# Two shifted bit patterns by one integer addition on GpSimd, in a two-block attention kernel

## The chip, the cores and the metric

The kernel runs on one core of one Trainium2 chip. The metric is the device time of one execution in microseconds. A core has TensorE (matrix products, written to PSUM), VectorE, ScalarE and GpSimd, each with its own queue of instructions worked off in order; they wait for each other by semaphores. DMAs are issued here from the queue of the sync engine. In the profile TensorE is PE (PEld is its loading of weights), VectorE is DVE, ScalarE is ACT, GpSimd is POOL and the sync engine is SP.

## The reference

Two attention blocks stand side by side. Both take x (2048 rows of 512) and weights in bfloat16, and have 32 heads of 16 channels. A is linear attention, B is full softmax attention. The two outputs are put together along the channels, to 2048 x 1024.

```python
def _A_ref(x, wqkv, wo):
    ...                                            # q, k, v: (B, H, S, Dh) from x @ wqkv
    phi = lambda t: jnp.where(t > 0, t + 1, jnp.exp(t)) + 1e-6
    pq, pk = phi(q), phi(k)
    kv = jnp.einsum("bhsd,bhse->bhde", pk, v)
    z = jnp.einsum("bhsd->bhd", pk)
    num = jnp.einsum("bhqd,bhde->bhqe", pq, kv)
    den = jnp.einsum("bhqd,bhd->bhq", pq, z)[..., None] + 1e-6
    o = num / den
    return (lambda x, *d: x.transpose(*d))(o, 0, 2, 1, 3).reshape(B, S, D) @ wo

def _B_ref(x, wqkv, wo):
    ...
    scores = jnp.einsum("bhqd,bhkd->bhqk", q, k) * scale     # scale = 16 ** -0.5
    p = _softmax(scores, axis=-1)
    o = jnp.einsum("bhqk,bhkd->bhqd", p, v)
    return (lambda x, *d: x.transpose(*d))(o, 0, 2, 1, 3).reshape(B, S, D) @ wo
```

B has by far the most work: 32 heads x 2048 x 2048 scores, each of which needs an exponential.

## The kernel before

The kernel is written as a planner. While the program is built, it keeps a clock for each engine, guesses how long each instruction takes (the numbers beside an engine's name, in us), and decides greedily which piece of work each engine does next. The order that comes out is fixed in the program; on the chip only semaphores hold it together. So a change of the guessed durations, or of which engine does what, gives another order and another division of the work.

B's scores are cut into blocks of 128 keys by 512 queries of one head. A unit is four heads (of one parity e_ within a group Gp of eight heads), one quarter of the queries, and all keys: 64 blocks. There are 32 units. Four heads' scores are made side by side in the array, 32 rows each. To take one head of a pair out of 32 rows, K lies masked: KM holds K with the rows of the other parity set to zero.

```python
    ABL = (3, 2)          # banks of the two PSUM tiles pS that ScalarE works on
    NDG = 4               # pattern buffers
    SHIFTS = (343, 685)
    VSCALE = (203.0 / 256.0, 161.0 / 256.0)
```

A block goes one of two ways. ScalarE takes three or two blocks in one exponential, from pS to PT (fp16):

```python
                    sch.add("act", lambda e: e.activation(PT[:, row, c0:c0 + w], SCR[sl][:, 0:w], ACTF.Exp, scale=SC),
                            reads=skeys(sl), writes=[("PT", row, sl)])
```

Or VectorE makes the exponential from bits: a multiply-add of a score from a bank of pD, converted to a 16-bit integer, read as fp16, is a rough exponential. Two more patterns, the same bits plus 343 and plus 685, multiplied by scaled copies of V (VSCALE), even out its error. So such a block has three products with V (vk is 0, 1, 2), and a block of ScalarE's has one.

```python
                    sch.add("dve", lambda e: e.tensor_scalar(DI[:, buf, 0, i * 512:(i + n) * 512], DB[:, bi * 512:(bi + n) * 512],
                                                             ESC, EB, op0=ALU.mult, op1=ALU.add), ...)
# ---- cut ----
            def shift(k_):
                def go(st_, en_):
                    sch.add("dve", lambda e: e.tensor_scalar(DI[:, buf, k_, 0:n * 512], DI[:, buf, 0, 0:n * 512], SHIFTS[k_ - 1], None, op0=ALU.add), ...)
# ---- cut ----
                        sch.add("pe", lambda e, g=g, vk=vk, c0=c0, P=P, first=first, last_=last_: e.matmul(
                            PVb[32 * g:32 * g + 17, 0:512], lhsT=VV[:, Gp % 2, vk, c0:c0 + 17], rhs=P,
                            start=first, stop=last_, tile_position=(0, 32 * g)), ...)
```

How many blocks go the second way is not fixed: the planner takes one whenever a bank of pD and a pattern buffer (DI) are free and VectorE's backlog is under 6 us.

```python
        def d_backlog(at):
            return max(0.0, T["dve"] - at) + sum(c_[3] for c_ in cands["dve"])
```

The masked K of all but the first head group is made by GpSimd from a copy (KR) of the projection:

```python
            st.append(("dve", 0.6, f_ev("dve", lambda e, bk: e.tensor_copy(KR[:, kr, :], f32v(bk)), [], [("KR", kr)])))
            for e_ in range(2):
                st.append(("pool", 1.7, f_op("pool", lambda e, e_=e_: e.tensor_scalar(KM[:, r, e_, cs], KR[:, kr, :], PAR[:, e_:e_ + 1], None, op0=ALU.mult), ...)))
```

At a unit's end VectorE transposes the products, takes the reciprocal of the sums and multiplies:

```python
            st = [("dve", 0.25, f_op("dve", lambda e: e.reciprocal(zr, o[:, :, 16]), ...)),
                  ("dve", 0.4, f_op("dve", lambda e: e.tensor_tensor(xn[:, :, 16 * e_:16 * e_ + 16], o[:, :, 0:16],
                                                                      zr.unsqueeze(2).broadcast_to([128, 16, 16]), op=ALU.mult), ...))]
```

A's work lies as small jobs between B's. Its K and V are made for 16 row tiles, in two halves of 256 columns each, and kept in KNa and VNa for the sums over the rows:

```python
                return e.matmul(f32v(bk)[:, 256 * k_:256 * k_ + 256], lhsT=xTa[:, cc, t * 128:(t + 1) * 128],
                                rhs=Wa[:, cc, 512 + 512 * k_ + 256 * hp:512 + 512 * k_ + 256 * hp + 256], start=(cc == 0), stop=(cc == 3))
```

Of the kernel before, what the change touches and what calls it, by code (L numbers as in the profile page):

```python
# [231 lines left out]
def bass_concat_heads__linear_attn_block__softmax_full_mha__prompt_kernel(nc, A_x, A_wqkv, A_wo, B_x, B_wqkv, B_wo, out):  # L232
# [4 lines left out]
    NT = S // 128  # L237
# [6 lines left out]
    NDG = 4  # L244
# [17 lines left out]
    with es:  # L262
# [12 lines left out]
        WOb = sb("WOb", [128, 4, 512], BF)  # L275
# [5 lines left out]
        DI = sb("DI", [128, NDG, 3, 1024], I16)  # L281
        KR = sb("KR", [128, 2, 512], BF)
        ON = sb("ON", [128, NT, 512], BF)
        KNa = sb("KNa", [128, NT, 256], BF)
        VNa = sb("VNa", [128, NT, 2, 129], BF)
# [67 lines left out]
        load(WOb[:], B_wo.rearrange("(c p) n -> p c n", p=128), ["WOb"])  # L353
# [25 lines left out]
        for r_ in range(2):  # L379
            sch.add("pool", lambda e, r_=r_: e.memset(  # L380
                VV[:, r_, 0, :].rearrange("p (h c) -> p h c", c=17)[:, :, 16:17], 1.0), writes=[("VV1", r_)])
        mk_ident(identf, "identf")
        band(BMk, 8, 16, "BMk")
        sch.add("pool", lambda e: e.memset(VNa[:, :, :, 128:129], 1.0), writes=["VNa1"])
# [49 lines left out]
        P1, SH = (0.61, 1.12), (0.21, 0.345)  # L434
        SLK = 0.0
        PVR, PVMIN, PVURG = 3, 6, 24
# [30 lines left out]
        krc = [0]  # L467

        def proj_job(Gp, sc, kind, fast=False, **kw):
            def mm(e, bk, cc):  # L470
                return e.matmul(f32v(bk), lhsT=Wb[:, cc, kind * 512 + Gp * 128:kind * 512 + Gp * 128 + 128],  # L471
                                rhs=xTb[:, cc, sc * 512:(sc + 1) * 512], start=(cc == 0), stop=(cc == 3))
            r = Gp % 2
            cs = slice(sc * 512, (sc + 1) * 512)
            st = halves(mm, [("Wb", kind, Gp)] + [("xTb", t) for t in range(4 * sc, 4 * sc + 4)])
            needs = [("xTb", t) for t in range(4 * sc, 4 * sc + 4)]
            if Gp >= 2:
                needs.append(("filled", Gp - 2))
            if kind == 0:
                st.append(("dve", 0.6, f_ev("dve", lambda e, bk: e.tensor_copy(QT[:, r, cs], f32v(bk)), [], [("QT", r, sc)])))  # L480
                return Job(st, needs, [(2, ("Q", Gp, sc))], rel=2, **kw)
            if fast:
                for e_ in range(2):
                    st.append(("dve", 0.66, f_ev("dve", lambda e, bk, e_=e_: e.tensor_scalar(KM[:, r, e_, cs], f32v(bk), PAR[:, e_:e_ + 1], None, op0=ALU.mult),  # L484
                                                 [("PAR", e_)], [("KM", r, e_, sc)])))
                return Job(st, needs, [(2, ("K", Gp, 0, sc)), (3, ("K", Gp, 1, sc))], rel=3, **kw)
            kr = krc[0] % 2
            krc[0] += 1
            st.append(("dve", 0.6, f_ev("dve", lambda e, bk: e.tensor_copy(KR[:, kr, :], f32v(bk)), [], [("KR", kr)])))  # L489
            for e_ in range(2):  # L490
                st.append(("pool", 1.7, f_op("pool", lambda e, e_=e_: e.tensor_scalar(KM[:, r, e_, cs], KR[:, kr, :], PAR[:, e_:e_ + 1], None, op0=ALU.mult),  # L491
                                             [("PAR", e_), ("KR", kr)], [("KM", r, e_, sc)])))
            return Job(st, needs, [(3, ("K", Gp, 0, sc)), (4, ("K", Gp, 1, sc))], rel=2, **kw)
# [81 lines left out]
        def akv_job(t, hp, **kw):  # L575
            def mm(e, bk, i):
                k_, cc = divmod(i, 4)
                return e.matmul(f32v(bk)[:, 256 * k_:256 * k_ + 256], lhsT=xTa[:, cc, t * 128:(t + 1) * 128],  # L578
                                rhs=Wa[:, cc, 512 + 512 * k_ + 256 * hp:512 + 512 * k_ + 256 * hp + 256], start=(cc == 0), stop=(cc == 3))
            st = halves(mm, ["Wa", ("xTa", t)], n=8, parts=2, dur=0.11)  # L580
            st += phi_stages(0, 256, KNa[:, t, :], [("KNa", t)])
            st.append(("dve", 0.34, f_ev("dve", lambda e, bk: e.tensor_copy(VNa[:, t, :, 0:128], f32v(bk)[:, 256:512].rearrange("p (b n) -> p b n", n=128)),
                                        [], [("VNa", t)])))
            return Job(st, [("xTa", t)] + ([("akv", hp - 1, bl) for bl in range(2)] if hp else []),
                       [(5, ("ak", hp, t))], **kw)

        def akvsum_job(hp, bl, **kw):
            bq = 2 * hp + bl
            def mm(e, bk, t):
                return e.matmul(f32v(bk, 129), lhsT=KNa[:, t, bl * 128:(bl + 1) * 128], rhs=VNa[:, t, bl, :], start=(t == 0), stop=(t == NT - 1))  # L590
            st = halves(mm, [("KNa", t) for t in range(NT)] + [("VNa", t) for t in range(NT)] + ["VNa1"], n=16, parts=4, dur=0.06)
            st.append(("dve", 0.25, f_ev("dve", lambda e, bk: e.tensor_tensor(RHA[:, bq, 0:128], f32v(bk, 128), BMk[:], op=ALU.mult), ["BMk"], [("RHA", bq)])))
            st.append(("dve", 0.15, f_ev("dve", lambda e, bk: e.tensor_tensor(
                RHA[:, bq, 128:136], ZMk[:], bk[0][:, bk[2] + 128:bk[2] + 129].broadcast_to([128, 8]), op=ALU.mult), ["ZMk"], [("RHZ", bq)])))
            return Job(st, [("ak", hp, t) for t in range(NT)], [(3, ("akv", hp, bl)), (5, ("rha", bq))], **kw)
# [47 lines left out]
        kst = lambda i: [("KNa", 2 * i), ("KNa", 2 * i + 1)]  # L643
        KNf = KNa[:, :, :].rearrange("p (s b) n -> p s (b n)", b=2)
# [3 lines left out]
        def omm_job(ab, t, o2, needs, gives, lane="dve", **kw):  # L648
# [5 lines left out]
            def fin(bk):  # L654
# [4 lines left out]
                       needs + ([("akv", 1, bl) for bl in range(2)] if o2 else []), gives, **kw)  # L659
# [47 lines left out]
        def qk_reads(bl):  # L707
            res = []
            for u, j, g in bl:
                Gp, c, e_ = unit(u)  # L710
                res += [("QT", Gp % 2, c), ("KM", Gp % 2, e_, j // 4)]
# [19 lines left out]
        def d_backlog(at):  # L731
            return max(0.0, T["dve"] - at) + sum(c_[3] for c_ in cands["dve"])

        grp = {"n": 0, "open": False}
# [64 lines left out]
        def shifts(buf):  # L799
# [5 lines left out]
            def shift(k_):  # L805
                def go(st_, en_):
                    sch.add("dve", lambda e: e.tensor_scalar(DI[:, buf, k_, 0:n * 512], DI[:, buf, 0, 0:n * 512], SHIFTS[k_ - 1], None, op0=ALU.add),  # L807
                            reads=[("DI", buf, 0, i) for i in range(n)], writes=[("DI", buf, k_, i) for i in range(n)])
                    for i in range(n):
                        done(buf, k_, i, en_)  # L810
                    if k_ == 1:
                        push("dve", en_, 1, SH[n - 1], shift(2))
                return go
            push("dve", s_["t"], 1, SH[n - 1], shift(1))
# [147 lines left out]
        def unit_done(u, t_):  # L962
# [9 lines left out]
                  ("dve", 0.4, f_op("dve", lambda e: e.tensor_tensor(xn[:, :, 16 * e_:16 * e_ + 16], o[:, :, 0:16],  # L972
# [60 lines left out]
        for hp in range(2):  # L1033
            for t in range(NT):
                ajobs.append(akv_job(t, hp))
            for bl in range(2):
                ajobs.append(akvsum_job(hp, bl))
# [52 lines left out]
        while True:  # L1090
# [12 lines left out]
            if fa is not None:  # L1103
                fao = pe_opt(fa[0], 0, fa[1], fa[2], None, "q")
                opts.append(fao)
            fd = fill_d_cand()
            if fd is not None:
                opts.append(pe_opt(fd[0], 3, fd[1], fd[2], None, "q"))
            elif not d_open():
                close_group()  # L1110
            lim = max(T["act"] + sum(exps) - fa[1] - PH - LAT - SLK, fa[0]) if fa is not None and nfill[0] >= 2 else None
# [108 lines left out]
```

## Time and profile before

| | |
|---|---|
| time, median of three runs | 790.32 us (789.88 to 794.22) |
| span of the profiled execution | 795.4 us |
| mean granted TensorE clock | 0.949 |

In a line of the page's costliest groups stand: the line of the source, the engine, the operation, what it writes and reads by the program's names (buffer numbers left out), the shapes, the count; then the busy time in us and the mean ns of one; then the idle time of the engine just before these instructions, and what ended most of it. pS and pD are the PSUM tiles of scores, pPV that of the products with V, PT ScalarE's exponentials, DI the bit patterns, VV the copies of V, OT, ZR and ON a unit's outputs, KNa, VNa, EA and PQT tiles of A. In a list of waits stand the engine and its instruction, whom it waited for, and the total us, the times and the longest us. L871 is ScalarE's exponential, L783 VectorE's multiply-add, L807 its two shifts, L704 the scores' matmuls, L946 the products with V, L491 GpSimd's masking of K.

The busy times of records that overlap are counted once, so a group's busy time is less than count times mean. The end of a matmul is modelled.

### The profile page before, as it was taken

To read this page: it belongs to the slowest core of one execution; us is meant where nothing else is said; L and a number is where in the kernel's file an instruction comes from. 1 tells how busy PE (TensorE), PEld (TensorE's weight loads), DVE (VectorE), ACT (ScalarE), POOL (GpSimd) and SP (SyncE) were. 2 spreads that over 40 slices of the span, in tenths; PEclk is the share of its full clock that TensorE was granted. 3 is DMA by queue.
4 is the path that set the end of the run, shared out by engine and by line. 5 is a ranking of instruction groups with operands and counts; after the bars stand their busy time and mean duration, and the time that the engine had idled before them with its cause. 6 is when DMAs were issued, how large, how long until landed. Compare 5 with 4: busy or idle time off the path is not lost.

```text
span 795.4 us, 14718 instructions
## 1 busy us (share of the span) xinstructions
PE 687.2 (86%) x6195; PEld 213.9 (27%) x6244; DVE 666.0 (84%) x1368; ACT 733.4 (92%) x679; POOL 43.2 (5%) x41
## 2 busy tenths in 40 slices
PE   7889988888889889888888888988888888888876
PEld 4234432222223333222223222222122222221211
DVE  5989897888978887999988799889778987877971
ACT  6999998899999997999999899979899988998894
POOL 1000011110000002210000001130000000000000
PEclk9999998999999999989999799999689999988996
DMA  9900000000000000000000000000000020000000
GB/s 202 222 2 1 2 1 1 2 1 1 2 1 1 1 2 1 1 14 15 21 7 1 15 23 18 1 8 21 14 14 1 8 47 22 7 27 1 28 1 31
DMA packets 32712, 15.69 MB, mean 20 GB/s; under 512 B 24960, under 2 KB 32128, under 8 KB 32640
## 3 DMA queue, kind: packets, MB, share of 16 engines
q1 hardware_dynamic: 31840, 14.29, 7.6%
q8 instruction: 51, 0.84, 0.5%
q10 hardware_dynamic: 800, 0.39, 0.2%
q14 instruction: 21, 0.17, 0.1%
HBM read 4.72 MB, written 4.19 MB: 11 GB/s over the span
## 4 chain that ended last, share of the span: by engine, by line
ACT 60%; PE 27%; DVE 10%; issue 1%; DMA 1%; SPq 1%; DVEq 0%
ACT PT L871 59%; PE pPV L946 9%; PE pS L704 7%; DVE DI L783 5%; PE pD L704 2%; DVE DI L807 2%; PE pD L471 2%; PE pD L578 2%; PE pD L652 2%; PE pD L599 1%; ACT EA L569 1%; DMA xTb<-in_B_x_dram 1%; PE pD L549 1%; SPq L342 1%; DVE PQT L572 0%
## 5 line engine op out<-in xcount | busy, mean ns | idle before, releaser
L871 ACT ACTIVATE PT<-pS 128x1536 f16<-128x1536 f32 x624 | 719.7, 1316 | 45.8 <-PE pD L704 27.6
L783 DVE TENSOR_SCALAR DI<-pD 128x512 int16<-128x512 f32 (+1 forms) x468 | 323.7, 708 | 59.0 <-PE pD L704 53.1
L704 PE MATMUL pS<-QT,KM 32*128 32x512 bf16 x1559 | 247.8, 399 | 69.5 <-ACT PT L871 65.4
L946 PE MATMUL pPV<-PT,VV 128*17 128x512 f16 x1559 | 249.4, 399 | 0.6 <-ACT PT L871 0.5
L946 PE MATMUL pPV<-DI,VV 128*17 128x512 f16 x1467 | 223.0, 400 | 2.2 <-DVE OT L966 1.8
L807 DVE TENSOR_SCALAR DI<-DI 128x1024 int16<-128x1024 int16 (+1 forms) x490 | 192.5, 424 | 5.0
L704 PE MATMUL pD<-QT,KM 32*128 32x512 bf16 x489 | 176.2, 396 | 10.3 <-DVE DI L783 7.0
L704 PEld LDWEIGHTS pS<-QT,KM 32*128 32x128 bf16 x1559 | 58.5, 91 | 287.0 <-ACT PT L871 236.4
L946 PEld LDWEIGHTS pPV<-PT,VV 128*17 128x17 bf16 x1559 | 50.6, 89 | 68.9 <-issue 56.4
L491 POOL TENSOR_SCALAR KM<-KR,PAR 128x512 bf16<-128x512 bf16 x24 | 39.5, 1657 | 491.1 <-DVE KR L489 477.9
L946 PEld LDWEIGHTS pPV<-DI,VV 128*17 128x17 bf16 x1467 | 45.9, 89 | 66.7 <-issue 46.0
L704 PEld LDWEIGHTS pD<-QT,KM 32*128 32x128 bf16 x489 | 40.9, 91 | 58.8 <-DVE DI L783 28.9
L966 DVE STREAM_TRANSPOSE OT<-pPV 128x512 f32<-128x512 f32 x32 | 22.8, 712 | 20.0 <-PE pPV L946 19.7
L578 PE MATMUL pD<-Wa,xTa 128*128 128x256 bf16 x256 | 37.7, 275 | 1.9 <-DVE DI L783 1.5
L471 PE MATMUL pD<-xTb,Wb 128*128 128x512 bf16 x104 | 32.3, 402 | 6.1 <-DVE DI L783 2.4
L569 ACT ACTIVATE EA<-pD 128x256 bf16<-128x256 f32 (+1 forms) x48 | 25.8, 538 | 0.0
L578 PEld LDWEIGHTS pD<-Wa,xTa 128*128 128x128 bf16 x256 | 20.4, 97 | 19.2 <-issue 8.5
L549 PE MATMUL pD<-Wb,xTb 128*128 128x128 bf16 x256 | 19.4, 223 | 2.3 <-DVE KM L484 1.0
L599 PE MATMUL pD<-xTa,Wa 128*128 128x512 bf16 x54 | 16.6, 388 | 2.7 <-DVE DI L783 1.4
L652 PE MATMUL pD<-WOa,ONT 128*128 128x512 bf16 x49 | 15.8, 396 | 3.2 <-issue 2.3
L549 PEld LDWEIGHTS pD<-Wb,xTb 128*128 128x128 bf16 x256 | 14.8, 99 | 9.9 <-issue 3.1
L652 PE MATMUL pD<-WOb,ON 128*128 128x512 bf16 x52 | 14.3, 407 | 3.4 <-DVE ON L977 2.7
(82 smaller groups left out, 259.1 us busy)
## 6 DMA issues: line engine op xcount, KB each, us to landing
out_dram<-OB SPq DMA_DIRECT2D x16, 128.0 KB, 1.7
out_dram<-KNa SPq DMA_DIRECT2D x16, 128.0 KB, 1.7
Wa<-in_A_wqkv_dram SPq DMA_DIRECT2D x1, 1536.0 KB, 8.3
Wb<-in_B_wqkv_dram SPq DMA_DIRECT2D x2, 384.0 KB, 5.4
Wb<-in_B_wqkv_dram SPq DMA_DIRECT2D x1, 512.0 KB, 4.5
WOb<-in_B_wo_dram SPq DMA_DIRECT2D x1, 512.0 KB, 9.2
WOa<-in_A_wo_dram SPq DMA_DIRECT2D x1, 512.0 KB, 10.0
ON<-in_B_x_dram ACTq DMA_DIRECT2D x1, 256.0 KB, 4.3
```

Source lines behind the costliest of these rows:

```text
L471: return e.matmul(f32v(bk), lhsT=Wb[:, cc, kind * 512 + Gp * 128:kind * 512 + Gp * 128 + 128], rhs=xTb[:, cc, sc * 512:(sc + 1) * 512], st ...
L491: st.append(("pool", 1.7, f_op("pool", lambda e, e_=e_: e.tensor_scalar(KM[:, r, e_, cs], KR[:, kr, :], PAR[:, e_:e_ + 1], None, op0=ALU.m ...
L549: return e.matmul(f32v(bk)[:, tl * 128:(tl + 1) * 128], lhsT=xTb[:, cc, t * 128:(t + 1) * 128], rhs=Wb[:, cc, 1024 + Gp * 128:1024 + Gp * ...
L569: ("act", 0.051 + n * 0.000833, f_ev("act", lambda e, bk: e.activation(EA[:, q, 0:n], f32v(bk)[:, c0:c0 + n], ACTF.Exp), [], [("EA", q)])),
L578: return e.matmul(f32v(bk)[:, 256 * k_:256 * k_ + 256], lhsT=xTa[:, cc, t * 128:(t + 1) * 128], rhs=Wa[:, cc, 512 + 512 * k_ + 256 * hp:51 ...
L599: return e.matmul(f32v(bk), lhsT=Wa[:, cc, bq * 128:(bq + 1) * 128], rhs=xTa[:, cc, sc * 512:(sc + 1) * 512], start=(cc == 0), stop=(cc == 3))
L652: return e.matmul(f32v(bk), lhsT=src, rhs=WO[:, hb, :], start=(hb == 0), stop=(hb == 3))
L704: return e.matmul(dst, lhsT=KM[32 * g:32 * g + 32, Gp % 2, e_, j * 128:(j + 1) * 128], rhs=QT[32 * g:32 * g + 32, Gp % 2, c * 512:(c + 1) ...
L783: sch.add("dve", lambda e: e.tensor_scalar(DI[:, buf, 0, i * 512:(i + n) * 512], DB[:, bi * 512:(bi + n) * 512], ESC, EB, op0=ALU.mult, op ...
L807: sch.add("dve", lambda e: e.tensor_scalar(DI[:, buf, k_, 0:n * 512], DI[:, buf, 0, 0:n * 512], SHIFTS[k_ - 1], None, op0=ALU.add), reads= ...
L871: sch.add("act", lambda e: e.activation(PT[:, row, c0:c0 + w], SCR[sl][:, 0:w], ACTF.Exp, scale=SC), reads=skeys(sl), writes=[("PT", row, ...
L946: sch.add("pe", lambda e, g=g, vk=vk, c0=c0, P=P, first=first, last_=last_: e.matmul(PVb[32 * g:32 * g + 17, 0:512], lhsT=VV[:, Gp % 2, vk ...
```

## The change

The change moves the two shifts from VectorE to GpSimd. A pair of 16-bit patterns lies in a 32-bit lane; one 32-bit integer addition of a constant that holds the shift twice adds it to both, as the patterns are positive and no carry crosses. One instruction makes both shifted copies of up to two blocks: the source is read twice by a broadcast, and the constants lie in the small tile SHC. It is there to free VectorE for more blocks, and so to take blocks off ScalarE.

GpSimd's earlier work is moved to make room: the masked K is now written by eight small DMAs of 16 partitions each, over zeros set once at the start. The multiplication at a unit's end goes to GpSimd. A's K and V are made in quarters of 128 columns, two row tiles at a time, so that KNa and VNa take half the room; B's output weights are loaded late into VNa's place. The room goes to six pattern buffers instead of four. The planner gets GpSimd's durations (1.17 us for one block's shifts, 2.05 for two), counts GpSimd's backlog as well, and has new priorities for what TensorE does next.

```diff
-    NDG = 4
+    NDG = 6
...
+        SHC = sb("SHC", [128, 4], I16)
-        KNa = sb("KNa", [128, NT, 256], BF)
-        VNa = sb("VNa", [128, NT, 2, 129], BF)
+        KNa = sb("KNa", [128, NT, 128], BF)
+        VNa = sb("VNa", [128, NT, 129], BF)
+        WOb = VNa[:, :, :].rearrange("p t n -> p (t n)")[:, 0:2048].rearrange("p (c n) -> p c n", n=512)
...
+        for e_ in range(2):
+            sch.add("pool", lambda e, e_=e_: e.memset(KM[:, 1, e_, :], 0.0), ...)
+        sch.add("pool", lambda e: e.memset(SHC[:, 0:2], SHIFTS[0]), writes=["SHC"])
+        sch.add("pool", lambda e: e.memset(SHC[:, 2:4], SHIFTS[1]), writes=["SHC"])
...
-        P1, SH = (0.61, 1.12), (0.21, 0.345)
+        P1, SH = (0.61, 1.12), (1.17, 2.05)
         SLK = 0.0
+        DEFER, FLOW, DPR, DDEL = 0.25, 3.5, 6, 0.0
...
-            for e_ in range(2):
-                st.append(("pool", 1.7, f_op("pool", lambda e, e_=e_: e.tensor_scalar(KM[:, r, e_, cs], KR[:, kr, :], PAR[:, e_:e_ + 1], None, op0=ALU.mult), ...)))
+            def ev(bk):
+                sch.add("dve", lambda e: e.tensor_copy(KR[:, kr, :], f32v(bk)), reads=[bk[3]], writes=[("KR", kr)])
+                for e_ in range(2):
+                    for q in range(4):
+                        p0 = 32 * q + 16 * e_
+                        sch.add(spread_lanes[4 * e_ + q], lambda e, e_=e_, p0=p0: e.dma_start(KM[p0:p0 + 16, r, e_, cs], KR[p0:p0 + 16, kr, :]), ..., queue="sp")
+                    tok[("K", Gp, e_, sc)] = T["dve"] + 4.0
...
-                return e.matmul(f32v(bk)[:, 256 * k_:256 * k_ + 256], lhsT=xTa[:, cc, t * 128:(t + 1) * 128],
-                                rhs=Wa[:, cc, 512 + 512 * k_ + 256 * hp:512 + 512 * k_ + 256 * hp + 256], start=(cc == 0), stop=(cc == 3))
+                return e.matmul(f32v(bk)[:, 128 * x:128 * x + 128], lhsT=xTa[:, cc, (t + i_) * 128:(t + i_ + 1) * 128],
+                                rhs=Wa[:, cc, c0:c0 + 128], start=(cc == 0), stop=(cc == 3))
...
         def d_backlog(at):
-            return max(0.0, T["dve"] - at) + sum(c_[3] for c_ in cands["dve"])
+            return max(max(0.0, T[k_] - at) + sum(c_[3] for c_ in cands[k_]) - sl for k_, sl in (("dve", 0.0), ("pool", 2.5)))
...
-            def shift(k_):
-                def go(st_, en_):
-                    sch.add("dve", lambda e: e.tensor_scalar(DI[:, buf, k_, 0:n * 512], DI[:, buf, 0, 0:n * 512], SHIFTS[k_ - 1], None, op0=ALU.add), ...)
+            def go(st_, en_):
+                w = 256 * n
+                sch.add("pool", lambda e: e.tensor_tensor(
+                    DI32[:, buf, 1:3, 0:w], DI32[:, buf, 0, 0:w].unsqueeze(1).broadcast_to([128, 2, w]),
+                    SHC32[:].unsqueeze(2).broadcast_to([128, 2, w]), op=ALU.add), ...)
...
-                  ("dve", 0.4, f_op("dve", lambda e: e.tensor_tensor(xn[:, :, 16 * e_:16 * e_ + 16], o[:, :, 0:16],
+                  ("pool", 0.65, f_op("pool", lambda e: e.tensor_tensor(xn[:, :, 16 * e_:16 * e_ + 16], o[:, :, 0:16],
...
+                have = sum(x is not None and x <= fa[0] + 0.05 for x in jfree[0:2])
+                want = min(2, 4 - ABL[nfill[0] % 2])
+                fao = pe_opt(fa[0], 0 if lim is None or fa[0] + DEFER > lim or have >= want or not d_open() else FLOW, fa[1], fa[2], None, "q")
...
-                opts.append(pe_opt(fd[0], 3, fd[1], fd[2], None, "q"))
+                opts.append(pe_opt(fd[0] + DDEL, DPR, fd[1], fd[2], None, "q"))
```

The last lines change the order on TensorE: the filling of ScalarE's banks may be put off a little when the two banks of pD are not free yet, so that both kinds of blocks go out together (a fill of three blocks takes one of VectorE's beside it, a fill of two takes two); a fill of pD by itself comes last.

## The prediction

> **What bounds the kernel now.** I read the page's first two parts, then the costliest groups, then who waits for whom, and last the timeline of single stretches.
>
> ```profile
> PE 687.2 (86%) x6195; PEld 213.9 (27%) x6244; DVE 666.0 (84%) x1368; ACT 733.4 (92%) x679; POOL 43.2 (5%) x41
> ...
> ACT  6999998899999997999999899979899988998894
> POOL 1000011110000002210000001130000000000000
> ```
>
> ScalarE is busy for 92% of the span and evenly so; no slice is idle on TensorE or VectorE either, and GpSimd is nearly empty. The kernel is a balance of three engines with ScalarE in front.
>
> ```profile
> L871 ACT ACTIVATE PT<-pS 128x1536 f16<-128x1536 f32 x624 | 719.7, 1316 | 45.8 <-PE pD L704 27.6
> L783 DVE TENSOR_SCALAR DI<-pD 128x512 int16<-128x512 f32 (+1 forms) x468 | 323.7, 708 | 59.0 <-PE pD L704 53.1
> L704 PE MATMUL pS<-QT,KM 32*128 32x512 bf16 x1559 | 247.8, 399 | 69.5 <-ACT PT L871 65.4
> ...
> L946 PE MATMUL pPV<-DI,VV 128*17 128x512 f16 x1467 | 223.0, 400 | 2.2 <-DVE OT L966 1.8
> L807 DVE TENSOR_SCALAR DI<-DI 128x1024 int16<-128x1024 int16 (+1 forms) x490 | 192.5, 424 | 5.0
> L704 PE MATMUL pD<-QT,KM 32*128 32x512 bf16 x489 | 176.2, 396 | 10.3 <-DVE DI L783 7.0
> ...
> L491 POOL TENSOR_SCALAR KM<-KR,PAR 128x512 bf16<-128x512 bf16 x24 | 39.5, 1657 | 491.1 <-DVE KR L489 477.9
> ```
>
> These give the split of the work. There are 2048 blocks of scores of 128 keys by 512 queries (32 units of 64). 1559 go through ScalarE's exponential: 719.7/1559 = 0.462 us of ScalarE each. 489 go through VectorE, which makes the bits of an fp16 exponential by one multiply-add (323.7/489 = 0.662 us each) and, per pair of blocks, two shifted copies (192.5/245 = 0.79 us per pair). Those blocks need three products with V instead of one: 1467 = 3 x 489.
>
> ```profile
> PEld pS L704 <- ACT PT L871: 236.4, 438, 1.5
> ...
> PE pS L704 <- ACT PT L871: 65.4, 149, 1.2
> DVE DI L783 <- PE pD L704: 53.1, 90, 2.5
> ...
> ACT PT L871 <- PE pD L704: 27.6, 26, 4.6
> ```
>
> TensorE stands before the next scores until ScalarE has emptied the bank, for 65 us in matmuls and up to 236 us if the weight loads' waits are counted; ScalarE stands for TensorE for only 45 us. So ScalarE sets the pace, and blocks taken off it are the only large gain. VectorE can't take them at 84%, unless it gives something up.
>
> **What the Trainium skill says.** "GPSIMD Engine Reference", section 4.1, says that an addition of two 32-bit integer tensors on GpSimd is an exact, wrapping integer addition; two 16-bit patterns can then go in one 32-bit lane as long as no carry crosses. No run so far shows it. Its section 3.1 gives 4497 ns for a two-input addition of 2048 elements; an estimate from that for the new instruction's 1024 outputs is 1024 x 4497/2048 = 2.25 us. The trace has only one GpSimd operation of this size, the masking of K, which takes a minimum of 1.56 us for 512 elements, 3.0 ns an element, so 2 ns an element is not unlikely. "SBUF — State Buffer", section "SBUF: two separate sides", says that GpSimd and a VectorE instruction that uses both ports lock each other out for a whole instruction. The trace of before agrees only in part:
>
> ```profile
> 148.50 0.75 DVE L807 TENSOR_SCALAR DI<-DI 128x1024 int16<-128x1024 int16 x2
> 149.45 0.69 DVE L783 TENSOR_SCALAR DI<-pD 128x512 int16<-128x512 f32 x1 [0.19 <-PE pD L704]
> 150.06 0.63 DVE L570 TENSOR_SCALAR EA<-EA 128x256 bf16<-128x256 bf16 x1
> 150.72 0.42 DVE L572 SCALAR_TENSOR_TENSOR KNa<-pD,EA 128x256 bf16<-128x256 f32 x1
> ```
>
> Two masking operations ran on GpSimd from 148.68 to 152.14. The SBUF-to-SBUF operation at 150.06 took 0.63 us where its group's mean is 0.23; the shifts before it, and what reads PSUM, lost nothing. Elsewhere GpSimd's operation grew from 1.56 to at most 1.98 us. So a meeting costs some 0.4 us on either side, not the whole 1.6 us.
>
> **The change part by part.**
> (a) The shifts leave VectorE: 245 pairs x 0.79 = 192.5 us less there. They come to GpSimd as one instruction per pair. The new plan reckons 2.05 us for it (a constant of the diff, 1.17 for a single block), the skill's estimate was 2.25; I take 2.1. At an unchanged number of blocks that is 245 x 2.1 = 515 us on GpSimd, which runs beside everything else. VectorE falls to 666 - 192.5 = 473 us.
> (b) The division of the attention outputs goes from VectorE (32 x 0.43 = 13.8 us) to GpSimd, which the plan reckons at 0.65 us: 32 x 0.65 = 21 us. VectorE: 460 us. It lies after a unit's last product and waits behind at most a shift or two; the next unit has some 24 us (790/32) of work before it needs the tile again. Off the path, but for about 1 us at the very end.
> (c) The masked K leaves GpSimd: 39.5 us less, for 12 x 8 = 96 small DMAs. Before, a masked K arrived 3.1 to 3.5 us after the copy; the plan allows 4.0 us for the DMAs, and K of the next head group is wanted tens of us later. Nothing on the path. Four more memsets at the start, estimated at 5 us on an idle GpSimd (128 f32 elements took 0.20 to 0.51 us), before its first addition.
> (d) A's K and V in quarters: the same columns (256 matmuls of 256 columns become 512 of 128) and the same number of exponentials and VectorE operations (32 groups of 256 + 256 columns in both). The 37.7 us of those matmuls stay near 40. Its use is the room: K, V and B's output weights shrink or share, and two more pattern buffers fit.
> (e) Six pattern buffers and the new priorities. A pair holds its buffer through the multiply-add (1.3 us), the shift (2.1 us where it was 0.8), and its six products. The longer hold is what the two buffers pay for.
> (f) The new balance. Let D be the number of blocks off ScalarE. ScalarE then works 0.462 x (2048 - D) + 13.7 us (the 13.7 is 733.4 - 719.7), GpSimd 1.05 x D + 29 us (2.1/2 per block, 21 for the division, 8 for setup), VectorE 460 + 0.662 x (D - 489). ScalarE and GpSimd meet where 1.512 x D = 930, D = 615: 675.6 and 674.8 us, and VectorE stands at 543. So about 126 blocks change sides, which takes 58 us off ScalarE.
> (g) TensorE pays 126 x 2 = 252 more products. Four run side by side in one step; twelve take 0.83 us in one stretch of the timeline and one takes 0.38, so a step is some 0.225 us, and 252/4 x 0.225 = 14 us. Some 126/2.5 = 50 fills of ScalarE's banks fall away, at 0.22 us of TensorE each: 11 us back. Its work hardly changes, but the span it has for it shrinks.
> (h) From busy to span. ScalarE is 92.2% busy now. With TensorE at nearly 690 us of busy time in a shorter span I don't expect 92% to hold; I take 90%: 675.6/0.90 = 751 us of span. The three timed runs have a median of 790.3 where the profiled span is 795.4, a ratio of 0.994: 746 us. I say **745 us**, 5.7% less.
>
> **The rivals.**
> 1. GpSimd becomes the bound. For it: the balance sends it to 675 of 751 us, it works strictly in order, and the masking operation's 3.0 ns an element is slower than the plan's 2.0. If an addition takes 2.4 us, at the plan's D it works 615 x 1.2 + 29 = 767 us, and TensorE, in order, stands before products that wait for a pattern: 775 to 790 us, all gain gone. Against it: the plan's constants for other engines are within 10% of the trace (0.61 us for the multiply-add against 0.66 measured).
> 2. TensorE becomes the bound. For it: 86% busy now, and its mean granted clock was 0.90 and 0.93 in the two stretches from 550 to 750 us against 0.98 before 400. If its 690 us can't be packed denser than 91%, the span is 758 and the time 754. Against it: a part of its busy time is a matmul's own 0.38 us from start to end, which overlaps the next when they follow closely.
> 3. The plan doesn't use the freed time: D stays near 489, because the two spare PSUM banks are also used by projections and by A. Then ScalarE still works 733 us, and the time stays at 785 to 790. For it: VectorE idled 53 us for scores already. Against it: the change raises the buffers and the order of fills for just that.
> 4. The lock. What remains on VectorE with SBUF on both sides, 48 + 32 operations of 0.23 to 0.31 us, meets GpSimd nearly always. At 0.4 us each that is 80 x 0.4 = 32 us of VectorE, which has the room (543 + 32 of 751); if each waits for a whole addition, 80 x 2 = 160 us and VectorE is at 94%: near 780 us.
>
> **Range and chances.** The middle case is 745. Rival 2 or a slightly slower addition gives 750 to 765, better packing of ScalarE at 92% with D = 640 gives (0.462 x 1408 + 13.7)/0.92 x 0.994 = 718. Eight in ten: 718 to 778. Within 2% means 774.5 to 806: rivals 1, 3 and the bad form of 4 lead there, 0.11 together. Slower than 806 needs GpSimd to stall TensorE worse than any of these sums: 0.05. Faster: 0.84.
>
> **What would show it.** Right: about 300 additions on GpSimd at 2.0 to 2.2 us spacing; products from patterns near 1850; the exponential's group at some 660 us in total and ScalarE still the busiest or level with GpSimd; VectorE near 75% or below; TensorE's waits for ScalarE smaller. Wrong: D below 540 (rival 3), TensorE waiting for GpSimd in the waits by tens of us or GpSimd over 95% busy (rival 1), the granted clock well under 0.93 and ScalarE waiting for TensorE by over 60 us (rival 2), the 0.23 us operations at over 1 us (rival 4). If ScalarE's own 0.462 us a block changes, step (f) is wrong at its root.

## The result, and the profile after

The changed kernel takes 765.42 us (median of 758.75 to 765.85) where the kernel before takes 790.32: a ratio of 0.9645, 95% interval 0.9551 to 0.9738. It is faster by 3.5%; the prediction said 745 us and 5.7%.

The first two parts of the page of the changed kernel:

```profile
span 763.6 us, 15402 instructions
...
PE 677.8 (89%) x6562; PEld 222.5 (29%) x6616; DVE 542.1 (71%) x915; ACT 708.0 (93%) x656; POOL 538.5 (71%) x327
...
DVE  5777876676676878767777697766777766767671
ACT  6899998999899999899999999998899987999894
POOL 4586565568686767567898688755788766879790
```

VectorE and GpSimd both stand at 71%, neither near its limit, and ScalarE is at 93% (92% before). So the freed time of VectorE was not turned into blocks as far as the engines would have allowed. The costliest groups say how far it went:

```profile
L891 ACT ACTIVATE PT<-pS 128x1536 f16<-128x1536 f32 (+1 forms) x601 | 693.2, 1297 | 35.1 <-PE pD L722 19.9
L827 POOL TENSOR_TENSOR DI<-DI,SHC 128x1024 int32<-128x1024 int32 x274 | 512.7, 1889 | 192.6 <-DVE DI L803 191.7
L803 DVE TENSOR_SCALAR DI<-pD 128x512 int16<-128x512 f32 (+1 forms) x537 | 360.2, 695 | 139.9 <-PE pD L722 129.7
L722 PE MATMUL pS<-QT,KM 32*128 32x512 bf16 x1501 | 240.5, 396 | 27.0 <-ACT PT L891 23.6
...
L966 PE MATMUL pPV<-DI,VV 128*17 128x512 f16 x1641 | 239.6, 393 | 2.8 <-DVE OT L986 2.7
L722 PE MATMUL pD<-QT,KM 32*128 32x512 bf16 x547 | 199.8, 397 | 24.6 <-DVE DI L803 13.8
...
L582 DVE TENSOR_SCALAR EA<-EA 128x256 bf16<-128x256 bf16 (+1 forms) x48 | 25.7, 535 | 16.5 <-ACT EA L581 16.0
```

547 blocks go off ScalarE now, 58 more than before, and not the 126 of the prediction. A block on ScalarE costs what it did (693.2/1501 = 0.462 us). GpSimd's addition takes 1.89 us, less than either estimate, and GpSimd idled 192 us, nearly all of it for VectorE's multiply-add, which itself idled 130 us for scores. The last line is A's minimum-and-add on VectorE. Its count is unchanged and its busy time has doubled. With the shapes kept apart, and with two other operations beside it, first before:

```profile
L977 DVE STREAM_TRANSPOSE ON<-OT 128x512 bf16<-128x512 bf16 x16 | 11.4, 710 | 0.5
...
L558 DVE TENSOR_SCALAR VV<-VV 128x544 bf16<-128x544 bf16 x32 | 8.4, 296 | 0.2
...
L570 DVE TENSOR_SCALAR EA<-EA 128x256 bf16<-128x256 bf16 x32 | 7.3, 229 | 2.9 <-ACT EA L569 2.7
L570 DVE TENSOR_SCALAR EA<-EA 128x512 bf16<-128x512 bf16 x16 | 5.0, 313 | 0.1
```

and now after:

```profile
L570 DVE TENSOR_SCALAR VV<-VV 128x544 bf16<-128x544 bf16 x32 | 16.6, 550 | 0.4
...
L582 DVE TENSOR_SCALAR EA<-EA 128x512 bf16<-128x512 bf16 x16 | 13.6, 848 | 5.0 <-ACT EA L581 4.7
...
L582 DVE TENSOR_SCALAR EA<-EA 128x256 bf16<-128x256 bf16 x32 | 12.1, 379 | 11.5 <-ACT EA L581 11.4
L997 DVE STREAM_TRANSPOSE ON<-OT 128x512 bf16<-128x512 bf16 x16 | 11.3, 705 | 3.5 <-POOL OT L992 3.5
```

All of these read and write SBUF. The three TENSOR_SCALAR groups grew; the transpose did not, though 13 of its 16 overlap an addition on GpSimd in time. So it is not every operation from SBUF to SBUF that suffers. One that does in the timeline, VectorE first, then GpSimd, TensorE and ScalarE:

```profile
319.23 0.69 DVE L803 TENSOR_SCALAR DI<-pD 128x512 int16<-128x512 f32 x1 [0.62 <-PE pD L722]
320.06 1.99 DVE L582 TENSOR_SCALAR EA<-EA 128x512 bf16<-128x512 bf16 x1
322.08 0.69 DVE L584 SCALAR_TENSOR_TENSOR PQT<-pD,EA 128x512 bf16<-128x512 f32 x1
```

```profile
320.00 1.89 POOL L827 TENSOR_TENSOR DI<-DI,SHC 128x1024 int32<-128x1024 int32 x1 [0.29 <-DVE DI L803]
```

```profile
322.83 0.38 PE L722 MATMUL pD<-QT,KM 32*128 32x512 bf16 x1 [1.45 <-DVE PQT L584]
```

```profile
319.38 0.65 ACT L581 ACTIVATE EA<-pD 128x512 bf16<-128x512 f32 x1
319.85 3.35 ACT L891 ACTIVATE PT<-pS 128x1024 f16<-128x1024 f32 x3
324.73 1.45 ACT L891 ACTIVATE PT<-pS 128x1536 f16<-128x1536 f32 x1 [1.53 <-PE pD L722]
```

The addition begins at 320.00 and ends at 321.89. VectorE's operation begins at 320.06 and ends at 322.05: it stood through the whole addition. This is no single case. Of A's 48 operations 19 began within an addition (the last of them 0.17 us before its end), and each of these ended 0.08 to 0.15 us after that addition, whether it had begun early or late in it; 16 began before the addition they overlap and kept their 0.22 to 0.29 us. The operation behind it, which is the one that frees the bank of pD, is late by that much; TensorE, in order, comes late to the next scores (it stood 1.45 us for L584), and ScalarE stands for 1.53 us at 324.73. VectorE's own wait stands in no list of waits: it is hidden in a duration. Only TensorE's wait behind it is listed, under L584: 6.3 us with a longest of 1.8, where it was 0.4 us in all before.

The stall reaches further. The next lines give a stretch, its length, then busy us of PE, PEld, DVE, ACT and POOL, then the granted clock, the DMA share and GB/s:

```profile
320.30:323.70 3.40, 1.74 (x8) 0.38 (x6) 3.37 (x4) 2.90 (x3) 1.60 (x1) 1.00 0.00 0
323.70:327.10 3.40, 3.40 (x23) 0.64 (x22) 2.38 (x5) 2.31 (x2) 1.95 (x2) 0.54 0.08 20
```

TensorE is busy for half of the first stretch, and in the second its clock is halved. In the clock records of these traces the granted clock is either full or half. The changed kernel has 11 stretches at half, 61 us together, and in the 3.4 us before each TensorE was busy for 43 to 84%, against 89% over the span. That a stall brings the clock down is suggested by this and not shown, as no run parts the two. It has to be kept in mind below, since in most comparisons the faster kernel also had the higher clock.

### The profile page after: what moved, and what is told of

The parts are those of the page before. It is cut to its first block, busy times and chain, and to the rows that moved or that the text cites. A ratio compares the mean times of both kernels' runs of the same rounds, so it can differ in the third digit from the quotient of the medians.

```text
span 763.6 us, 15402 instructions
## 1 busy us (share of the span) xinstructions
PE 677.8 (89%) x6562; PEld 222.5 (29%) x6616; DVE 542.1 (71%) x915; ACT 708.0 (93%) x656; POOL 538.5 (71%) x327
## 4 chain that ended last, share of the span: by engine, by line
ACT 58%; PE 29%; DVE 10%; issue 1%; POOL 0%; POOLq 0%
ACT PT L891 57%; PE pPV L966 10%; PE pS L722 7%; DVE DI L803 4%; PE pD L722 3%; DVE EA L582 2%; PE pD L477 2%; PE pD L670 2%; PE pD L592 2%; ACT EA L581 1%; PE pD L561 1%; DVE VV L570 1%; PE pD L617 1%; PE pD L520 1%; DVE PQT L584 1%
## 5 line engine op out<-in xcount | busy, mean ns | idle before, releaser
L891 ACT ACTIVATE PT<-pS 128x1536 f16<-128x1536 f32 (+1 forms) x601 | 693.2, 1297 | 35.1 <-PE pD L722 19.9
L827 POOL TENSOR_TENSOR DI<-DI,SHC 128x1024 int32<-128x1024 int32 x274 | 512.7, 1889 | 192.6 <-DVE DI L803 191.7
L803 DVE TENSOR_SCALAR DI<-pD 128x512 int16<-128x512 f32 (+1 forms) x537 | 360.2, 695 | 139.9 <-PE pD L722 129.7
L966 PE MATMUL pPV<-DI,VV 128*17 128x512 f16 x1641 | 239.6, 393 | 2.8 <-DVE OT L986 2.7
L722 PE MATMUL pD<-QT,KM 32*128 32x512 bf16 x547 | 199.8, 397 | 24.6 <-DVE DI L803 13.8
L592 PE MATMUL pD<-Wa,xTa 128*128 128x128 bf16 x512 | 38.7, 225 | 0.8 <-DVE DI L803 0.4
L582 DVE TENSOR_SCALAR EA<-EA 128x256 bf16<-128x256 bf16 (+1 forms) x48 | 25.7, 535 | 16.5 <-ACT EA L581 16.0
L992 POOL TENSOR_TENSOR OT<-OT,ZR 128x256 bf16<-128x256 f32 x32 | 20.0, 625 | 22.3 <-DVE ZR L991 22.2
L592 PEld LDWEIGHTS pD<-Wa,xTa 128*128 128x128 bf16 x512 | 30.1, 100 | 15.3 <-DVE DI L803 8.2
L670 PE MATMUL pD<-VNa,ON 128*128 128x512 bf16 x50 | 13.9, 382 | 3.8 <-DVE ON L997 2.8
```

The costliest lines, as they stand in the source:

```text
L582: ("dve", 0.067 + n * 0.00026, f_op("dve", lambda e: e.tensor_scalar(EA[:, q, 0:n], EA[:, q, 0:n], 1.0, 1e-6, op0=ALU.min, op1=ALU.add), [ ...
L592: return e.matmul(f32v(bk)[:, 128 * x:128 * x + 128], lhsT=xTa[:, cc, (t + i_) * 128:(t + i_ + 1) * 128], rhs=Wa[:, cc, c0:c0 + 128], star ...
L670: return e.matmul(f32v(bk), lhsT=src, rhs=WO[:, hb, :], start=(hb == 0), stop=(hb == 3))
L722: return e.matmul(dst, lhsT=KM[32 * g:32 * g + 32, Gp % 2, e_, j * 128:(j + 1) * 128], rhs=QT[32 * g:32 * g + 32, Gp % 2, c * 512:(c + 1) ...
L827: sch.add("pool", lambda e: e.tensor_tensor(DI32[:, buf, 1:3, 0:w], DI32[:, buf, 0, 0:w].unsqueeze(1).broadcast_to([128, 2, w]), SHC32[:]. ...
```

## The theories and the experiments

**A**: ScalarE's blocks set the time, however they are got rid of. **B**: the gain is that of the six buffers and the priorities, and the addition on GpSimd adds little. **C**: what counts is VectorE's freedom. **D**: TensorE's products stand behind patterns that come late from GpSimd. **Port**: GpSimd's additions hold up VectorE's SBUF operations, and through them pD, TensorE and ScalarE. Ratios are to the kernel before, intervals are of 95%.

**a1, the changed kernel again.** No edit.

> The changed kernel once more, as the yardstick beside the others: 0.9645 of the kernel before, so 758 to 766 us. Every theory expects the same.

764.93 us (762.79 to 767.36), ratio 0.9641 [0.9581, 0.970]. It is the yardstick below. The runs of a, b and c were made on three chips, where the kernel before took 792.77, 791.17 and 792.37 us.

**a2, the shifts back on VectorE, everything else of the change kept.**

```diff
-        P1, SH = (0.61, 1.12), (1.17, 2.05)
+        P1, SH = (0.61, 1.12), (0.21, 0.345)
-                sch.add("pool", lambda e: e.tensor_tensor(DI32[:, buf, 1:3, 0:w], ..., op=ALU.add), ...)
+                sch.add("dve", lambda e: e.tensor_scalar(DI[:, buf, k_, 0:n * 512], DI[:, buf, 0, 0:n * 512], SHIFTS[k_ - 1], None, op0=ALU.add), ...)
```

> The whole change except its title: the two shifts go back to VectorE, six buffers, new priorities, K by DMAs and the division on GpSimd stay. The planner then puts 520 blocks off ScalarE (547 in the changed kernel, 489 before). Theory A (ScalarE's blocks set the time, however they are got rid of): ScalarE works 0.462 x 1528 + 15 = 721 us; at 93% busy a span of 775 us, a time near 774, ratio 0.98. Theory B (the gain is that of the buffers and priorities, and GpSimd's addition adds little): 765 to 770, ratio about 0.97. Theory C (VectorE's freedom is what counts): VectorE near 88% and TensorE in order behind it, 785 to 790, ratio 0.995 to 1.0.

759.62 us (758.92 to 763.1), ratio 0.9581 [0.9522, 0.9641]. Without its title the change is at least as good. C falls outright, and A alone too, since 519 blocks off ScalarE (the expectation's 520 takes a single block for a pair) do no worse than 547, at a like clock (0.960 to 0.966, in a1 0.960 to 0.969). The page of this kernel:

```profile
PE 660.8 (87%) x6560; PEld 215.5 (28%) x6560; DVE 670.0 (88%) x1401; ACT 718.0 (95%) x667; POOL 28.5 (4%) x53
...
L891 ACT ACTIVATE PT<-pS 128x1536 f16<-128x1536 f32 x612 | 705.4, 1315 | 21.6 <-PE pD L722 15.6
```

ScalarE works 10 us more than in the changed kernel, but idles 757.4 - 718.0 = 39 us where it idled 763.6 - 708.0 = 56. So with the additions on GpSimd ScalarE stands 16 us longer, although VectorE is less busy (71% against 88%); the shares of busy time don't tell why.

**a3, four buffers in the changed kernel.**

```diff
-    NDG = 6
+    NDG = 4
```

> The changed kernel with four pattern buffers instead of six and nothing else changed. The planner then puts only 422 blocks off ScalarE. Theory A: ScalarE works 0.462 x 1626 + 15 = 766 us; at 92 to 93% busy 825 to 830 us, slower than the kernel before by 4 to 5%, though VectorE has lost all its shifts. If the buffers matter little on the chip (a rival that says the planner is too pessimistic of them): no more than 790.

839.75 us, ratio 1.058 [1.0516, 1.0644]: slower than expected even by A. Part of it is the planner's own; two stretches, with the columns explained above:

```profile
80.00:240.00 160.00, 130.53 (x969) 38.21 (x963) 38.26 (x88) 141.83 (x132) 18.20 (x13) 0.68 0.02 4
240.00:839.00 599.00, 518.97 (x4675) 155.28 (x4674) 367.71 (x583) 555.65 (x511) 359.30 (x209) 0.94 0.06 14
```

From 80 to 240 us VectorE works 38 of 160 us: the planner put hardly any block off ScalarE there, and the granted clock fell to 0.68. So the run shows that this order can't live with four buffers, not what four buffers cost as such. b1 asks that in a cleaner way.

**a4, half of each addition.** Only the first shifted pattern is made, both products read it, the second is left out.

```diff
-                    DI32[:, buf, 1:3, 0:w], DI32[:, buf, 0, 0:w].unsqueeze(1).broadcast_to([128, 2, w]),
-                    SHC32[:].unsqueeze(2).broadcast_to([128, 2, w]), op=ALU.add),
+                    DI32[:, buf, 1:2, 0:w], DI32[:, buf, 0, 0:w].unsqueeze(1).broadcast_to([128, 1, w]),
+                    SHC32[:, 0:1].unsqueeze(2).broadcast_to([128, 1, w]), op=ALU.add),
```

> The order of the changed kernel kept, but each addition on GpSimd makes only the first shifted pattern, and both products read that one; the second pattern is left out. GpSimd's work falls from 538 to about 290 us. Theory A (GpSimd is off the path, at 71% busy): within 1% of the changed kernel, 757 to 768. Rival D (products stand behind GpSimd's 1.9 us additions in TensorE's order): lower by 10 us or more, and VectorE's 0.38 and 0.85 us operations of A back at 0.23 and 0.31 in either case if they meet a busy GpSimd less often.

745.07 us, ratio 0.9409 [0.9342, 0.9476]: 20 us less than a1 in the same order. GpSimd idles more than half of the span, and yet its length matters; A's "off the path at 71% busy" is wrong.

```profile
L827 POOL TENSOR_TENSOR DI<-DI,SHC 128x512 int32<-128x512 int32 x274 | 283.8, 1038 | 370.9 <-DVE DI L803 370.5
```

An addition of 1.04 us leaves VectorE's three operations at 0.26, 0.48 and 0.34 us on average. By its time D and Port both fit. D does not fit the waits, for in the changed kernel TensorE's products wait for the additions for 0.7 us in all:

```profile
PEld pPV L966 <- POOL DI L827: 0.7, 3, 0.2
```

b2 and b4 try the two theories.

**b1, the six buffers alone.** The kernel before, with its planner's order of fills, its shifts and division on VectorE and K masked by GpSimd, and only the buffers and the room for them (quarters of A, B's output weights late). The memsets at the start and the count of GpSimd's backlog stay in too.

```diff
-    NDG = 4
+    NDG = 6
-        KNa = sb("KNa", [128, NT, 256], BF)
-        VNa = sb("VNa", [128, NT, 2, 129], BF)
+        KNa = sb("KNa", [128, NT, 128], BF)
+        VNa = sb("VNa", [128, NT, 129], BF)
+        WOb = VNa[:, :, :].rearrange("p t n -> p (t n)")[:, 0:2048].rearrange("p (c n) -> p c n", n=512)
```

> The kernel before with six pattern buffers and the room for them (A in quarters, B's output weights late), and nothing else of the change: shifts and division on VectorE, masked K by GpSimd, the old order of fills. The planner puts 518 blocks off ScalarE instead of 489. If the buffers carry the gain (theory B): 0.462 x 1530 + 14 = 721 us of ScalarE at 94 to 95%, span 760 to 767, ratio 0.96 to 0.97, no worse than the whole change. If the new priorities or the division on GpSimd carry it: 780 or more, ratio above 0.985.

768.51 us, ratio 0.9723 [0.9664, 0.9782]. That is just above the range expected. The buffers alone bring 2.8%, nearly four fifths of the whole change's gain. With them the planner finds 518 blocks, and VectorE, at 84% before, does 89%:

```profile
PE 662.6 (87%) x6505; PEld 220.1 (29%) x6558; DVE 682.7 (89%) x1442; ACT 720.0 (94%) x667; POOL 47.3 (6%) x45
```

So VectorE at 84% was not full; it was short of buffers. The other parts without the title (order of fills, division, K by DMAs: a2 against b1) bring a further 0.9723 to 0.9581.

**b2, the port kept clear of A's operation.** The changed kernel's order; the operation is computed in another place. exp(x) stays in EA; the maximum is taken in PSUM in place, and the minimum moves into the next operation. The function is the same.

```diff
-  e.tensor_scalar(EA[:, q, 0:n], EA[:, q, 0:n], 1.0, 1e-6, op0=ALU.min, op1=ALU.add)
+  e.tensor_scalar(f32v(bk)[:, c0:c0 + n], f32v(bk)[:, c0:c0 + n], 0.0, 1e-6, op0=ALU.max, op1=ALU.add)
-  e.scalar_tensor_tensor(out_ap, f32v(bk)[:, c0:c0 + n], 0.0, EA[:, q, 0:n], op0=ALU.max, op1=ALU.add)
+  e.scalar_tensor_tensor(out_ap, EA[:, q, 0:n], 1.0, f32v(bk)[:, c0:c0 + n], op0=ALU.min, op1=ALU.add)
```

> The changed kernel in the same order, but A's minimum-and-add on VectorE, which reads and writes SBUF, is replaced by a maximum-and-add in place in PSUM (the minimum moves to the operation behind it; the same function is computed). If GpSimd's additions cost time because this operation stands behind them (0.38 and 0.85 us instead of 0.23 and 0.31, up to 2 us, with a PSUM bank held): ScalarE's idle time falls from 55 us towards 40, time 748 to 757, although VectorE gets some 12 us more work. If they cost it through the patterns arriving late (theory D): unchanged, 760 to 768.

749.35 us, ratio 0.9453 [0.9398, 0.9509]: 15.6 us less than a1. The operation, with its shapes kept apart:

```profile
L582 DVE TENSOR_SCALAR pD<-pD 128x256 f32<-128x256 f32 x32 | 13.7, 428 | 11.2 <-ACT EA L581 11.1
L582 DVE TENSOR_SCALAR pD<-pD 128x512 f32<-128x512 f32 x16 | 11.1, 696 | 5.2 <-ACT EA L581 5.0
```

It costs 24.8 us in all, hardly less than the 25.7 of the changed kernel, so VectorE gained nothing. What went is the long tail: 0.70 us is its longest now, it was 1.99. ScalarE's idle time fell to 752.9 - 708.1 = 45 us. GpSimd's additions are the same 274 of 1.89 us. D expected no change. Part of the gain may come by way of the clock, which was 0.975 to 0.989 here and 0.960 to 0.969 in a1. The one run of the changed kernel with a like clock (0.977) took 758.75 us, b2's with 0.975 and 0.979 took 754.68 and 750.64: 4 to 8 us less, from three single runs.

**b4, one product instead of three.** For the blocks off ScalarE only the product with the first pattern is made; those with the two shifted patterns are left out.

```diff
+                        if vk == 0 or first or last_:
                           sch.add("pe", ...)
```

> The changed kernel's order with two of the three products with V left out for nearly every block off ScalarE (those that open or close a sum are kept), so about 1,080 of 3,142 products less on TensorE, about 60 us of its steps; GpSimd's additions still run, but nothing on TensorE reads them. If TensorE bounds the kernel or its waits for the patterns do: 735 or less. If ScalarE and VectorE's chain set it: 750 to 762. It also bounds what theory D can be worth: a product can't stand behind an addition that no product reads.

770.68 us, ratio 0.9744 [0.9686, 0.9801]. 547 products with patterns are left of 1641, and the time is, if anything, 0.8% longer than a1's, outside both ranges expected. No product reads a shifted pattern here, so the wait of D can't arise, and nothing was gained by that. With the 0.7 us of waits above, D falls. What the products themselves cost TensorE stays open: its clock was 0.936 to 0.947 here and 0.960 to 0.969 in a1. In the profiled runs that is 0.938 and 0.969, or some 95 and 47 us at half clock, as (1 - 0.938) x 2 x 769.5 and (1 - 0.969) x 2 x 762.8, and the lower clock may hide a gain. Why it was lower I can't say, and no run tells.

**c1, the control of b2: its edit with the shifts on VectorE** (the edit of b2 on the kernel of a2).

> The same edit of A's minimum-and-add as in b2, but with the shifts on VectorE (the kernel of a2, 759.6 us, ratio 0.958), where GpSimd runs only 32 short multiplications. If b2's gain is the meeting with GpSimd's additions: no gain here, 757 to 768, as VectorE only gets some 12 us more work. If the edited operation is simply better (it reads PSUM, frees the bank in the same way, or saves a wait): some 12 to 15 us less, 745 to 750.

773.81 us, ratio 0.9752 [0.9682, 0.9822], against 759.62 for a2: 14 us more, above both ranges expected. Where GpSimd makes no additions the edit is a loss; where it makes them it is a gain of 16. So the gain of b2 is in the meeting of the two and not in the operation. The control isn't perfect, as the edit adds VectorE's work here and none in b2; but a4, which leaves the operation alone and shortens the additions, points the same way. Some 13 us more of VectorE's work came with 14 us of time, but the clock was lower too (0.945 to 0.953, in a2 0.960 to 0.966), so what each of them cost is open.

**c2, shorter exponentials.** Of the 2560 columns of each pair of exponentials 192 are left out, so 7.5% of ScalarE's probabilities and not the eighth that the expectation names.

```diff
-  e.activation(PT[:, row, c0:c0 + w], SCR[sl][:, 0:w], ACTF.Exp, scale=SC)
+  e.activation(PT[:, row, c0:c0 + (w * 448 // 512 + 64)], SCR[sl][:, 0:(w * 448 // 512 + 64)], ACTF.Exp, scale=SC)
```

> The changed kernel's order with ScalarE's exponentials shortened: 1408 and 960 columns instead of 1536 and 1024, the products reading blocks that overlap by 64 columns (an eighth of the probabilities is left out). At 0.83 ns a column that takes 0.16 us off each pair of exponentials, 48 us in all. If ScalarE still sets the pace: 765 falls by 30 to 45 us, to 720 to 735. If VectorE's chain and TensorE's order set it as much: 745 or more.

730.96 us, ratio 0.9226 [0.9159, 0.9293]. ScalarE's work fell from 708 to 668 us, the time by 34 us of those 40. So ScalarE still sets the pace in the changed kernel, and work taken off it and put nowhere else pays 85% (at a clock of 0.974 to 0.981). In c2 itself it hardly does any more: it has 21% of the chain that ended last and TensorE 55%, where they had 58% and 29% in the changed kernel.

**b3 and c4, the port kept clear, planned anew; c3, their rival.** b3 is b2 with the planner told the operation's new duration, and settings found by a search for the shortest plan. c4 also makes the two scaled copies of V from PSUM. c3 is a2 with the same kind of search.

```diff
 b3
-    DNEXT, DEND, TEND, ALAG, DLEAD = 16, 20, 720.0, 20.0, 0.5
+    DNEXT, DEND, TEND, ALAG, DLEAD = 8, 8, 760.0, 25.0, 1.2
-        SLK = 0.0; DEFER = 0.25; PVURG = 24
+        SLK = -0.1; DEFER = 0.3; PVURG = 28
 c4, beyond b2's edit
-  ("dve", 0.21, ... e.tensor_scalar(v[k_ + 1], v[0], VSCALE[k_], None, op0=ALU.mult), ...)
+  ("dve", 0.6, ... e.tensor_scalar(v[k_ + 1].rearrange("p (h c) -> p h c", c=17)[:, :, 0:16], f32v(bk).rearrange("p (h d) -> p h d", d=16), VSCALE[k_], None, op0=ALU.mult), ...)
+  (the copies' 17th column is set once to VSCALE; DNEXT 12, DEND 14, TEND 735, ALAG 25, SLK -0.1, FLOW 2.1, PVMIN 7, PVURG 28)
 c3
-    DEND, DLEAD = 20, 0.5;  DEFER, FLOW = 0.25, 3.5
+    DEND, DLEAD = 8, 1.2;   DEFER, FLOW = 0.3, 4.5
```

> As b2, with the planner told the new duration and its settings for the end of units and the order of A's work searched for the shortest plan (556 blocks off ScalarE). Theory of the port: 0.462 x 1492 + 15 = 704 us of ScalarE at 94.5%, a span of 745, time 745 to 752, ahead of both kernels and of the shifts on VectorE (759.6). Theory D: no better than the changed kernel.

> The kernel of a2 (shifts on VectorE) with the same search of the planner's settings as b3 had: 530 blocks off ScalarE, VectorE at nearly 90%. It is the fair rival of b3. 0.462 x 1518 + 15 = 716 us of ScalarE at 94.5% is a span of 758: 752 to 760. If it reaches 746 as b3, GpSimd's addition brings nothing even with the port kept clear.

> As b3, and the two scaled copies of V are made from PSUM too, with their column of constants set once at the start (0.30 us operations that stretched to 0.55, now some 0.69 that never meet GpSimd); settings searched anew, 542 blocks off ScalarE. If the port's cost was A's operation alone: 750 to 755, no better than b3. If V's share counts: 740 to 746.

| | us, median (range) | ratio, 95% interval | blocks off ScalarE | ScalarE idle, us |
|---|---|---|---|---|
| b3 | 746.01 (743.9 to 751.9) | 0.9448 [0.9381, 0.9515] | 556 | 41 |
| c3 | 750.68 (749.75 to 752.97) | 0.9481 [0.9413, 0.9548] | 530 | 35 |
| c4 | 740.94 (739.78 to 742.75) | 0.9356 [0.9289, 0.9423] | 542 | 31 |

c4 is the best version of all and beats both kernels. Its page:

```profile
PE 654.4 (89%) x6552; PEld 222.1 (30%) x6606; DVE 541.6 (73%) x906; ACT 707.1 (96%) x658; POOL 536.5 (73%) x328
...
L893 ACT ACTIVATE PT<-pS 128x1536 f16<-128x1536 f32 x603 | 694.0, 1304 | 13.3 <-PE pD L724 8.3
```

Before its exponentials ScalarE idles 13 us where the changed kernel has 35. With the port clear of A's operation and of V's copies the addition on GpSimd is worth something after all: 740.9 against 750.7, on the same chip, with ranges that don't touch; the ratios' intervals overlap a little. It is the best plan found of each kind that is compared, each with its own settings. b3 against c3 is within the noise. c4 has two edits over b2 (V's copies and the settings), and no run parts them.

## Why the prediction was right in direction and 20 us too low

The time lies in the range and the side is right; the steps in the prediction's own order:

- (a) The addition was put at 2.1 us and measured 1.89 (two in a row take 3.74), so it was put too high by 11%. GpSimd worked 538 us and not 675; about half of that difference is the blocks that didn't come (68 x 1.05 = 71 us). Without effect on the sum, since D stayed far below where GpSimd is full. VectorE's 542 us look like the 543 predicted, but that is luck: at 547 blocks the prediction's sum gives 460 + 0.662 x 58 = 498. Of the 44 us between, 22 are the operations that grew (rival 4). Most of the rest comes from how busy time is counted: VectorE's groups sum to 715 us before and overlap by 49, now to 566 and overlap by 24.
- (b) The division takes 0.62 us on GpSimd (0.65 assumed), and VectorE waited for it 3.5 us in all. Right.
- (c) The 96 DMAs land after 1.8 us at the median; the eight issues of one K take 5.0 us in the queue, so K is complete some 7 us after the copy, not 4. Nobody waits for it. Right in effect.
- (d) A's matmuls: 38.7 us against 37.7. Right.
- (e) The buffers were named as what pays for the longer hold. That undersold them: b1 shows that they bring 2.8% with no shift moved at all.
- (f) **This step failed.** It let D rise until ScalarE and GpSimd met, at 615. D came to 547. 68 blocks x 0.462 = 31 us of ScalarE's work that stayed, 35 us of time at its 90%. What holds D back is for the most part not GpSimd: it idled 192 us for VectorE, and VectorE 130 us for scores in pD. The planner's own count agrees: told that a pair's shifts take 0.5 us instead of 2.05 it puts 554 blocks off ScalarE, told that the multiply-add takes 0.40 us for one block and 0.70 for two it puts 569, and with four buffers 421 (a3). D hangs on how fast a bank of pD comes round, by TensorE's order and the multiply-add, and on buffers. (These are counts of the plan; of them only a3 was run.)
- (g) TensorE's busy time was to stay near 690; it is 678. Right. Whether the added products were rightly called cheap isn't shown: b4 left 1094 products out and gained nothing, but at a lower clock.
- (h) ScalarE was to be 90% busy; it is 708.0/763.6 = 92.7%. This gave back most of what (f) lost: (0.462 x 1501 + 13.7)/0.90 = 786 us, at 92.7% 763. The rest is the profiled run, which this time isn't longer than the timed ones (763.6 to 765.4, a ratio of 1.002 for the 0.994 used): 6 us.
- Rival 4, the lock: its size was of the right order and its meaning wrong. 80 operations of VectorE grew by 25.7 - 12.3 + 16.6 - 8.4 = 21.6 us together (32 predicted), which was set aside because VectorE "has the room". But A's operation holds a bank of pD and stands in front of the next multiply-add, so what VectorE had to spare didn't help: b2 gets back 15.6 us of time, part of it perhaps through the clock.
- The sign that pointed there was in the prediction's own timeline, the 0.63 us operation. From "0.4 us a meeting" I went to a sum over an engine's free time and not to who waits behind that operation. In the Trainium skill, "SBUF — State Buffer", section "SBUF: two separate sides" says that the loser "fully blocks" for the whole instruction. The addition of the changed kernel agrees with it (0.31 us became 1.99, against an addition of 1.89, and 19 operations that ended just after an addition); I had taken the milder reading from the masking operation.
- Rival 3 was right in kind: about half of the freed time was used. Rival 1 is refuted by GpSimd's 71% and the 0.7 us of waits. Of rival 2's signs none came: the clock was 0.960, and ScalarE waited for TensorE's scores for 19.9 + 14.3 = 34 us and not for over 60.

The account of the gain, by ratios: buffers and room 0.972; order of fills, division and K by DMAs 0.958; the addition on GpSimd, which gives the change its title, 0.964, so nothing or a small loss (the intervals of a1 and a2 overlap); with A's operation out of its way 0.945, part of that perhaps through the clock.

## What to carry to other kernels

Before moving work from VectorE to GpSimd, list what stays on VectorE with both ends in SBUF, and ask for each who waits behind it: such an operation can grow by a whole GpSimd instruction, and on VectorE it shows only as a longer duration, never as a wait. Compare durations by shape, since not all grow (the transposes here did not). An operand in PSUM, even at twice the time, can be the cheaper form beside a busy GpSimd; beside one without additions it was a loss (c1). Write the granted clock beside each time, as a stall and a lower clock can come together. And where a change makes room for buffers and also moves work, run the buffers alone first: they may be the gain.

## What the runs showed of the hardware that was not expected

- A 32-bit integer addition on GpSimd with 1024 outputs and both inputs broadcast takes 1.89 us, with 512 outputs 1.04: 1.66 ns an element and 0.19 us besides. The estimate from the Trainium skill's 4497 ns for 2048 elements ("GPSIMD Engine Reference", section 3.1) was 2.25.
- Two thirds of the products with patterns left out saved no time (b4), at a lower granted clock.
- In the stretch of a3 where few blocks went off ScalarE the granted clock was 0.68, against 0.94 in the rest; what lowered it was not tested.
